# K projection of a DiT block: one more matmul ahead of two scale groups, and two K steps batch by batch

## The chip, the cores and the metric

The kernel runs on one core of a Trainium2 chip. The metric is device time in microseconds (us). "Span" is the time from the first to the last instruction in a profile; the timed figure is about 1.8 us longer (243.07 for a span of 241.26 in the profile of the kernel before).

## The reference, cut to what matters

```
B, N, D = 2, 256, 1152;  F = 4 * D                 # bf16
mod = (silu(c) @ w_mod).reshape(B, 6, 1, D)        # shift_a, scale_a, gate_a, shift_m, ...
h   = layernorm(x) * (1 + scale_a) + shift_a
qkv = (h @ wqkv)                                   # q, k, v;  2 heads of 576
...                                                # attention, wo, gate, second layernorm, MLP
```

Only the first microseconds matter here: `scale_a` is a small product of `silu(c)` with 1152 columns of `w_mod`, then the K projection needs `layernorm(x) * (1 + scale_a)`, transposed, as its moving operand. The shift is added later.

## The kernel before: the parts that the change touches

Tokens of both batches stand side by side: 512 columns, batch 0 in the first 256, batch 1 in the rest. The contraction of 1152 is cut into nine K steps of 128. Six PSUM accumulators `pk[0..5]` are filled step by step. The scale comes in groups of columns (0, 1, 2-3, 4-5, 6-7, 8), each from its own load.

```python
    for k0, k1 in SGROUPS:            # (0,2) (2,4) (4,6) (6,8) (8,9)
        nc.sync.dma_start(w_scale_a[...k0:k1...], ...)         # weights of the scale
        for a, z in [(0, 1), (1, 2)] if k0 == 0 else [(k0, k1)]:
            load_k(a, z, 0, KM1 * P)                           # weights of K, same rows
    load_k(0, KD, KM1 * P, D)
    # ... then w_shift_a, w_q, all on one queue
# [...]
    def scale_group(k0, k1, ...):     # 9 matmuls of 2 columns for each of the group's 128-column blocks
    def scale_add(pm, k0, k1, ...):   # VectorE: scale_a = pm + 1
    def both(pt, k):                  # scale the transposed block: batch 0 VectorE, batch 1 ScalarE
        for b, e in enumerate("da"):
            modulate(pt, 0, k, b, b * N, e)
    def k_step(k, c0=0, c1=T, m0=0, m1=KM1):
        for m in range(m0, m1):       # K step k, columns c0:c1, accumulators m0..m1-1
            nc.tensor.matmul(pk[m][:, c0:c1], w_k[:, k, m * P:(m + 1) * P], hT0[:, k, c0:c1], ...)
# [...]  K steps 0 to 2, scale groups 0 to 2-3
    for k in range(3, KD):
        split = 2 if k in (3, 5) else 0
        k_step(k, 0, T, 0, split)
        if k in (3, 5, 7):
            k1 = min(k + 3, KD)
            scale_add(scale_group(k + 1, k1), k + 1, k1)
        if k < KD - 1:
            both(transpose_x([k + 1], range(NT)), k + 1)
        k_step(k, 0, T, split)
# [...]  the last three column blocks of K, the shift, Q, attention, MLP
```

So the order on TensorE is: two matmuls of step 3, scale group 4-5, transposes of block 4, four matmuls of step 3, transposes of block 5, step 4, two matmuls of step 5, scale group 6-7, and so on.

## Time and profile before

| | |
|---|---|
| time, when the prediction was made | 242.99 us median of 3 (242.89 to 243.03) |
| span | 241.3 us |
| TensorE busy | 236.3 us, 98% |
| chain that ended last | 95% TensorE |

The page of the profile of before. The busy row of TensorE (PE), the clock in tenths over 40 slices, and the chain of waits that ended last:

```profile
span 241.3 us, 3993 instructions
...
PE 236.3 (98%) x1698; PEld 144.6 (60%) x1698; DVE 91.6 (38%) x194; ACT 60.1 (25%) x122; POOL 28.3 (12%) x47
...
PEclk9999999999999999999999999999999999999999
...
PE 95%; DMA 2%; DVE 1%; SPq 0%; issue 0%; DVEq 0%
```

A TensorE that is 98% busy is not necessarily without bubbles (short stretches in which the array has nothing to stream), because records of matmuls overlap: one of 512 columns is recorded as 379 ns long, but the next starts 216 ns later. What counts is the distance between starts. The timeline of TensorE in the kernel before (start in us, length in us, engine, line, what, how often) shows it. L250 are the scale groups, L267 transposes, L282 K steps:

```profile
9.30 0.60 PE L250 MATMUL pm<-sT,w_scale_a 128*128 128x2 bf16 x18
...
12.47 0.59 PE L250 MATMUL pt<-sT,w_scale_a 128*128 128x2 bf16 x18
...
15.44 0.59 PE L250 MATMUL pm<-sT,w_scale_a 128*128 128x2 bf16 x18
15.89 0.38 PE L267 MATMUL pt<-ident,xn 128*128 128x128 bf16 x4
16.11 1.03 PE L282 MATMUL pk<-big,w_k 128*128 128x512 bf16 x4
16.98 0.39 PE L267 MATMUL pt<-ident,xn 128*128 128x128 bf16 x4
17.25 1.89 PE L282 MATMUL pk<-big,w_k 128*128 128x512 bf16 x8
19.10 0.60 PE L250 MATMUL pm<-sT,w_scale_a 128*128 128x2 bf16 x18
19.56 0.38 PE L267 MATMUL pt<-ident,xn 128*128 128x128 bf16 x4
19.78 1.03 PE L282 MATMUL pk<-big,w_k 128*128 128x512 bf16 x4
20.64 0.39 PE L267 MATMUL pt<-ident,xn 128*128 128x128 bf16 x4
20.92 1.46 PE L282 MATMUL pk<-big,w_k 128*128 128x512 bf16 x6
22.21 0.37 PE L250 MATMUL pm<-sT,w_scale_a 128*128 128x2 bf16 x9
```

From 17.25 to 19.10 there are eight matmuls of 216 ns: 1.73 us of work in 1.85 us, so 0.12 us are lost ahead of group 6-7. Four transposes need 4 x 55 ns; from 16.98 to 17.25 and from 20.64 to 20.92 is 0.27 us, so 50 ns are lost ahead of K steps 4 and 6. What they wait for is told by the weight loads (PEld) of the same lines:

```profile
15.37 0.57 PEld L250 LDWEIGHTS <-w_scale_a 128*128 128x128 bf16 x18 [0.26 <-DMA w_scale_a<-in_w_mod_dram]
19.09 0.52 PEld L250 LDWEIGHTS <-w_scale_a 128*128 128x128 bf16 x18 [0.45 <-DMA w_scale_a<-in_w_mod_dram]
```

Both groups' weight loads wait for a transfer, but only the second wait costs the array anything: at 15.37 the matmul before it was still streaming.

The view of one load's line gives its issue and landing. For the load of group 6-7 in the kernel before:

```profile
L109 SPq DMA_DIRECT2D w_scale_a<-in_w_mod_dram x1: 469/469/469, 11.1 to 11.1; - x1
...
DMA to landing us min/median/max: 7.9/7.9/7.9
```

Issued at 11.1 us and landed 7.9 us later, at 19.05. (The trace has these in ns; 19.050.)

The waits at K steps 4 and 6 are for ScalarE, which scales batch 1 behind VectorE's batch 0:

```profile
16.34 0.35 DVE L273 TENSOR_SCALAR big<-pt,scale_a 128x256 bf16<-128x256 bf16 x1
```

```profile
16.72 0.47 ACT L274 ACTIVATE big<-pt,scale_a 128x256 bf16<-128x256 bf16 x1 [2.53 <-DVE big L273]
```

ScalarE starts 30 ns after VectorE ends, though it needs nothing that VectorE writes. Both read the same PSUM tile. The Trainium skill, "PSUM — Partial Sum Buffer", section "PSUM bank collisions raise a hardware error", says that no two engines may read one bank and quadrant at the same time and that schedulers put a dependency between them; the trace agrees here (16.69 to 16.72), and where the two batches lie in two tiles, at 13.30 and 13.36, the engines do overlap. Whether the wait is put in by tile or by bank, the trace doesn't tell.

### The profile page before, as it was taken

Reading aid. Unit: us, or ns where it says so; the run is one execution under the profiler, and the core shown is the slowest. Engines: PE = TensorE matmul, PEld = TensorE weight load, DVE = VectorE, ACT = ScalarE, POOL = GpSimd, SP = SyncE. Lnnn points to the kernel's source line nnn. Section 1 sums busy time; section 2 is a strip of 40 time slices with the busy share of each in tenths; the row PEclk is TensorE's granted clock in tenths of the full one; section 3 lists DMA queues with packets and bytes.
Section 4 is the critical chain, followed back from the end, with each engine's and each line's share of the span. In section 5 each row is a group of like instructions: output and inputs, shape, how many; then the busy total and the mean of one; then the engine's idle time right before and its main releaser. Section 6 shows DMA issues by size and latency. Waiting matters only on the chain.

```text
span 241.3 us, 3993 instructions
## 1 busy us (share of the span) xinstructions
PE 236.3 (98%) x1698; PEld 144.6 (60%) x1698; DVE 91.6 (38%) x194; ACT 60.1 (25%) x122; POOL 28.3 (12%) x47
## 2 busy tenths in 40 slices
PE   8899999999999999999999999999999999999994
PEld 5675444466667566888844444444666656666674
DVE  4842442319325678930002999950000000000001
ACT  6732322307215032770423333222000000000000
POOL 2300000001400324100000000001121111111111
PEclk9999999999999999999999999999999999999999
DMA  6999999998599994739999999999300000000000
GB/s 196 324 317 311 376 367 391 389 393 249 99 315 397 387 311 81 196 62 364 390 392 392 339 326 284 285 326 275 98 16 16 20 16 16 19 18 18 26 25 16
DMA packets 48925, 53.30 MB, mean 221 GB/s; under 512 B 9731, under 2 KB 36619, under 8 KB 48907
## 3 DMA queue, kind: packets, MB, share of 16 engines
q1 hardware_dynamic: 41312, 50.14, 62.6%
q10 hardware_dynamic: 7083, 1.72, 4.9%
q0 software_dynamic: 512, 1.19, 2.2%
q8 instruction: 13, 0.21, 0.4%
q14 instruction: 5, 0.04, 0.1%
HBM read 50.15 MB, written 1.19 MB: 213 GB/s over the span
## 4 chain that ended last, share of the span: by engine, by line
PE 95%; DMA 2%; DVE 1%; SPq 0%; issue 0%; DVEq 0%
PE pacc L806 29%; PE pacc L750 29%; PE pacc L697 7%; PE pacc L603 7%; PE pq L525 7%; PE pk L282 5%; PE pk L311 2%; DMA x_sb<-in_x_dram 2%; PE pa L644 2%; PE ps_s L560 2%; PE pn L420 2%; PE pt L267 1%; PE pm L250 1%; DVE stats L195 1%; PE pg L502 0%; SPq L88 0%
## 5 line engine op out<-in xcount | busy, mean ns | idle before, releaser
L750 PE MATMUL pacc<-hT,w_f 128*128 128x256 bf16 (+1 forms) x432 | 70.5, 326 | 0.0
L806 PE MATMUL pacc<-w_f,gT 128*128 128x384 bf16 (+2 forms) x468 | 70.5, 314 | 0.0
L806 PEld LDWEIGHTS <-gT 128*128 128x128 bf16 x468 | 44.4, 98 | 26.2
L750 PEld LDWEIGHTS <-w_f 128*128 128x128 bf16 x432 | 42.2, 98 | 27.6
L812 DVE TENSOR_TENSOR tmp<-pacc,gate 128x384 f32<-128x384 f32 (+2 forms) x13 | 6.9, 527 | 65.6 <-PE pacc L806 57.3
L782 ACT ACTIVATE gT<-pacc 128x512 bf16<-128x512 f32 x24 | 14.3, 597 | 32.7 <-PE pacc L750 32.7
L473 DVE SCALAR_TENSOR_TENSOR part<-w_gate_m,s,part 128x1152 f32<-128x1152 bf16 x16 | 21.4, 1414 | 0.0
L814 POOL TENSOR_TENSOR o_sb<-tmp,x 128x384 bf16<-128x384 f32 (+1 forms) x12 | 11.6, 971 | 53.9 <-DVE tmp L812 53.9
L697 PE MATMUL pacc<-w_o,big 128*128 128x384 bf16 x108 | 17.9, 326 | 0.0
L525 PE MATMUL pq<-hT,w_q 128*128 128x512 bf16 x81 | 17.8, 379 | 0.0
L603 PE MATMUL pacc<-w_v,hT 128*128 128x384 bf16 x108 | 17.7, 326 | 0.0
L603 PEld LDWEIGHTS <-hT 128*128 128x128 bf16 x108 | 10.5, 98 | 7.1 <-issue 0.3
L697 PEld LDWEIGHTS <-big 128*128 128x128 bf16 x108 | 10.4, 98 | 7.2 <-issue 0.4
L525 PEld LDWEIGHTS <-w_q 128*128 128x128 bf16 x81 | 7.9, 98 | 9.4
L282 PE MATMUL pk<-big,w_k 128*128 128x256 bf16 (+1 forms) x72 | 13.2, 325 | 0.0
L703 POOL TENSOR_TENSOR x<-tmp,x_sb 128x384 f32<-128x384 f32 x8 | 7.3, 911 | 26.3 <-DVE tmp L702 26.3
L471 DVE TENSOR_SCALAR part<-w_gate_m,s 128x1152 f32<-128x1152 bf16 x2 | 1.6, 818 | 22.2 <-DMA w_gate_m<-in_w_mod_dram 22.2
L495 POOL DMA_DIRECT2D gates_dram<-nat_v x2 | 1.1, 534 | 67.7 <-DVE nat_v L493 67.7
L282 PEld LDWEIGHTS <-w_k 128*128 128x128 bf16 x72 | 6.8, 97 | 3.5 <-issue 0.2
L771 ACT ACTIVATE gT<-pacc 128x512 bf16<-128x512 f32 x12 | 6.5, 597 | 9.1 <-PE pacc L750 9.1
L516 POOL DMA_DIRECT2D gates_dram<-nat x4 | 2.4, 596 | 49.8 <-DVE nat L513 48.4
L175 PE MATMUL pwarm<-zeros 128*128 128x256 f32 x18 | 6.7, 540 | 1.2 <-DVE eps_t L95 1.2
(106 smaller groups left out, 164.4 us busy)
## 6 DMA issues: line engine op xcount, KB each, us to landing
w_f<-in_w_fc_dram SPq DMA_DIRECT2D x12, 864.0 KB, 14.2
w_f<-in_w_fc_dram SPq DMA_DIRECT2D x3, 1728.0 KB, 10.1
w_f<-in_w_fc_dram SPq DMA_DIRECT2D x2, 2592.0 KB, 17.2
w_gate_a<-in_w_mod_dram SPq DMA_DIRECT2D x3, 864.0 KB, 14.4
w_v<-in_wqkv_dram SPq DMA_DIRECT2D x3, 864.0 KB, 15.4
w_o<-in_wo_dram SPq DMA_DIRECT2D x3, 864.0 KB, 14.7
w_shift_m<-in_w_mod_dram SPq DMA_DIRECT2D x3, 864.0 KB, 9.5
w_scale_m<-in_w_mod_dram SPq DMA_DIRECT2D x3, 864.0 KB, 15.8
```

The costliest lines, as they stand in the source:

```text
L175: nc.tensor.matmul(dst[:, 0:T // 2], zeros32[:, 0:P], zeros32, start=True, stop=True)
L282: nc.tensor.matmul(pk[m][:, c0:c1], w_k[:, k, m * P:(m + 1) * P], hT0[:, k, c0:c1], start=(k == 0 and c0 == 0), stop=(k == KD - 1), skip_g ...
L473: nc.vector.scalar_tensor_tensor(part[:, b, :], wg[:, k, :], s32[:, k, b:b + 1], part[:, b, :], op0=ALU.mult, op1=ALU.add,)
L525: nc.tensor.matmul(pq[m][:], w_q[:, k, m * P:(m + 1) * P], hT[:, k, :], start=(k == 0), stop=(k == KD - 1), skip_group_check=True,)
L603: nc.tensor.matmul(pacc[:], hT[:, k, t * P:(t + 1) * P], w_v[:, k, pnl * PW:(pnl + 1) * PW], start=(k == 0), stop=(k == KD - 1),)
L697: nc.tensor.matmul(pacc[:], aT[:, k, t * P:(t + 1) * P], w_o[:, k, c0:c1], start=(k == 0), stop=(k == KD - 1),)
L703: (nc.gpsimd if pool_add else nc.vector).tensor_tensor(x1[:, t, c0:c1], tmp[:], x_sb[:, t, c0:c1], op=ALU.add)
L750: nc.tensor.matmul(dst, w_f1[m // KD][:, k, ml * P:(ml + 1) * P], hT[:, k, c0:c1], start=start, stop=(k == KD - 1), **kw,)
L782: nc.scalar.activation(gT[:, m, :], pacc[:], ACT.Gelu_apprx_tanh)
L806: nc.tensor.matmul(pacc[:], gT[:, kk, t * P:(t + 1) * P], w_f2[j][:, r, c0 - n * PW:c0 - n * PW + cw], start=(kk == 0), stop=(kk == KF - 1),)
L812: nc.vector.tensor_tensor(tmp[:], pacc[:], gate_m[:, b, c0:c0 + cw], op=ALU.mult)
L814: (nc.vector if last else nc.gpsimd).tensor_tensor(o_sb[:], tmp[:], x1[:, t, c0:c0 + cw], op=ALU.add)
```

## The change

The intent: a third matmul of 216 ns goes ahead of groups 4-5 and 6-7, to cover the wait for their weights. That moves the scaling of the next block 216 ns closer to its use, so K steps 4 and 6 are cut in two: first all six accumulators for batch 0, which VectorE has ready early, then all six for batch 1.

```diff
     for k in range(3, KD):
-        split = 2 if k in (3, 5) else 0
+        split = 3 if k in (3, 5) else 0
         k_step(k, 0, T, 0, split)
         if k in (3, 5, 7):
             k1 = min(k + 3, KD)
             scale_add(scale_group(k + 1, k1), k + 1, k1)
         if k < KD - 1:
             both(transpose_x([k + 1], range(NT)), k + 1)
-        k_step(k, 0, T, split)
+        for c0, c1 in ((0, N), (N, T)) if k in (4, 6) else ((0, T),):
+            k_step(k, c0, c1, split)
```

## The prediction

> **What bounds the kernel now.** TensorE. The page gives PE 236.3 us busy of a 241.3 us span; the chain that ended last is 95% PE, 2% DMA, 1% DVE. The clock is full in all slices. Busy time hides bubbles, so I read starts of single matmuls in the timeline: a 512-column matmul starts 216 ns after its predecessor, a 256-column one 109-110 ns. This agrees with the Trainium skill, "TensorE: Matmul & The Clock Gate", section "Wait — 56ns, not 53.3ns?": columns / 2.4 GHz plus about 2.5 ns. Only three bubbles of K steps 3 to 8 can be won:
>
> - K step 4 starts at 17.25, 105 ns after the last transpose (55 ns is normal): its first matmul takes all 512 tokens and waits for ScalarE's scaling of batch 1, over at about 17.2. Loss about 50 ns.
> - Scale group 6-7 starts at 19.10, 341 ns after its predecessor (216 normal): its weights landed at 19.05. Loss 125 ns, and 10 ns in its first steps.
> - K step 6 starts at 20.92, as step 4: about 51 ns.
>
> Group 4-5 loses nothing: landed at 15.33, it started at 15.44, 216 ns after its predecessor; the 0.26 us idle shown there is of the weight load.
>
> **What the change does.**
> 1. One more 512-column matmul (216 ns) goes ahead of groups 4-5 and 6-7, one less follows. Work is moved, none added. Before 6-7 it covers the DMA wait: the group is then ready at about 19.16, behind the landing (19.05). Saves about 0.135 us. Before 4-5 there is nothing to cover.
> 2. Alone that would hurt K steps 4 and 6: scale add, VectorE scaling (0.35 us), then ScalarE scaling (0.47 us) come 216 ns later against TensorE, so batch 1 of step 4 is ready at about 17.45, against 17.20 for the array. Batch by batch, the first six matmuls need batch 0 alone (VectorE done at about 16.9) and run 0.66 us, when batch 1 has long been ready. Both 50 ns waits go.
> 3. The split makes twelve 256-column matmuls of six 512-column ones, twice: 6 x (2 x 109.2 - 215.8) = about 16 ns per step. The added weight loads of 98 ns hide behind 109 ns.
>
> Sum: -0.135 - 0.10 + 0.03 = about -0.2 us by scale group 8 (22.21 before, about 22.01 after).
>
> **Is it on the critical path?** Yes. Later loads land before they are needed: columns 6-8 of w_k at 24.57 (needed 25.03; slack 0.42 after the 43 ns from landing to load), first part of w_shift_a at 28.79 (needed 29.22; slack 0.39), w_q at 31.07 (needed 31.70). All exceed 0.2. From 30 us on TensorE has no wait over 0.1 us left, so the tail moves earlier whole. The loads before 30 us don't depend on TensorE.
>
> **Predicted: 242.80 us**, 8 in 10 within 242.60 to 243.05. Faster by over 2%: 0.5%; within 2%: 99%; slower: 0.5%.
>
> **Signs.** Right: scale group 6-7 begins 216 ns after its predecessor, without a wait for DMA; K steps 4 and 6 begin about 55 ns after the last transpose; PE has 1710 matmuls; span about 241.1. Wrong: a wait at batch 1, weight loads that show (over 110 ns per 256-column matmul), or a new DMA wait at w_k or w_shift_a.
>
> **What would make it wrong:** transfers landing 0.2 us later, which gives the gain back at 25 or 29 us; noise between runs (0.14 us) as large as the gain.

## The result

| | before | after |
|---|---|---|
| median (range), 6 executions each | 243.01 us (242.89 to 243.35) | 243.21 us (242.83 to 243.31) |
| span of the profile | 241.3 us | 241.4 us |

The ratio of after to before is 1.0003, with a 95% interval of 0.999 to 1.0016: the same. The predicted 242.80 us, and its range up to 243.05, were missed.

The page of after:

```profile
span 241.4 us, 4017 instructions
...
PE 235.6 (98%) x1710; PEld 145.3 (60%) x1710; DVE 91.5 (38%) x194; ACT 60.2 (25%) x122; POOL 28.3 (12%) x47
...
PE 95%; DMA 3%; SPq 1%; DVE 0%; issue 0%; DVEq 0%
```

TensorE has twelve more matmuls and 0.7 us less of recorded busy time, and yet the span is 0.1 us longer. The timeline of TensorE in after, for the same stretch and the start of the kernel:

```profile
9.58 0.60 PE L250 MATMUL pm<-sT,w_scale_a 128*128 128x2 bf16 x18 [0.27 <-DMA w_scale_a<-in_w_mod_dram]
...
12.83 0.59 PE L250 MATMUL pt<-sT,w_scale_a 128*128 128x2 bf16 x18
...
16.02 0.59 PE L250 MATMUL pm<-sT,w_scale_a 128*128 128x2 bf16 x18
16.47 0.38 PE L267 MATMUL pt<-ident,xn 128*128 128x128 bf16 x4
16.69 0.81 PE L282 MATMUL pk<-big,w_k 128*128 128x512 bf16 x3
17.34 0.39 PE L267 MATMUL pt<-ident,xn 128*128 128x128 bf16 x4
17.56 2.12 PE L282 MATMUL pk<-big,w_k 128*128 128x256 bf16 x15
19.52 0.59 PE L250 MATMUL pm<-sT,w_scale_a 128*128 128x2 bf16 x18
19.97 0.38 PE L267 MATMUL pt<-ident,xn 128*128 128x128 bf16 x4
20.19 0.81 PE L282 MATMUL pk<-big,w_k 128*128 128x512 bf16 x3
20.84 0.39 PE L267 MATMUL pt<-ident,xn 128*128 128x128 bf16 x4
21.06 1.47 PE L282 MATMUL pk<-big,w_k 128*128 128x256 bf16 x12
```

All three bubbles are gone. From 17.34 to 17.56 and from 20.84 to 21.06 is 0.22 us: four transposes and no wait. From 17.56 to 19.52 are twelve matmuls of 109 ns and three of 216 ns, 1.96 us of work in 1.96 us. The first matmul of scale group 8 started at 22.37, 22.21 in before. Everything else in this stretch starts later than in before, because the stretch itself began later: scale group 2-3 stands at 12.83, not 12.47. The weight loads of groups 4-5 and 6-7 in after wait for nothing:

```profile
15.80 0.72 PEld L250 LDWEIGHTS <-w_scale_a 128*128 128x128 bf16 x18
19.30 0.71 PEld L250 LDWEIGHTS <-w_scale_a 128*128 128x128 bf16 x18
```

The view of the load of group 6-7 in after:

```profile
L109 SPq DMA_DIRECT2D w_scale_a<-in_w_mod_dram x1: 470/470/470, 11.5 to 11.5; - x1
...
DMA to landing us min/median/max: 7.2/7.2/7.2
```

It was issued 0.37 us later than in before and landed 0.31 us earlier, at 18.74. So even without the change, group 6-7 would not have waited in this execution.

That suggests cutting each execution into three parts:

- **head**: from the start of the span to the first matmul of scale group 2-3. The two programs are the same up to here.
- **stage**: from there to the first matmul of scale group 8. The whole change lies here.
- **tail**: the rest.

| in ns, from the traces | head | stage | tail | span |
|---|---|---|---|---|
| before | 12469 | 9741 | 219054 | 241264 |
| after | 12830 | 9543 | 219054 | 241427 |

The tail is the same to the nanosecond. The stage is 198 ns shorter; the prediction had said 0.2 us. The head, which the change doesn't touch, is 361 ns longer. Of this, 274 ns are there already at scale group 0, which waited for its weights in after (the bracket at 9.58 above) and started at 9.30 in before: they landed at 9.15 in before and at 9.53 in after. The rest comes ahead of two transposes that wait for the normalised tile of x whose load landed last (7.21 in before, 7.57 in after).

### The profile page after: what moved, and what is told of

It reads as the page before. It is cut to its first block, busy times and chain, and to the rows that moved or that the text cites. A ratio compares the mean times of both kernels' runs of the same rounds, so it can differ in the third digit from the quotient of the medians.

```text
span 241.4 us, 4017 instructions
## 1 busy us (share of the span) xinstructions
PE 235.6 (98%) x1710; PEld 145.3 (60%) x1710; DVE 91.5 (38%) x194; ACT 60.2 (25%) x122; POOL 28.3 (12%) x47
## 4 chain that ended last, share of the span: by engine, by line
PE 95%; DMA 3%; SPq 1%; DVE 0%; issue 0%; DVEq 0%
PE pacc L807 29%; PE pacc L751 29%; PE pacc L698 7%; PE pacc L604 7%; PE pq L526 7%; PE pk L282 5%; DMA w_scale_a<-in_w_mod_dram 3%; PE pk L311 2%; PE pa L645 2%; PE ps_s L561 2%; PE pn L421 2%; PE pt L267 1%; PE pm L250 1%; SPq L88 1%; PE pg L503 0%; PE pt L250 0%
## 5 line engine op out<-in xcount | busy, mean ns | idle before, releaser
L282 PEld LDWEIGHTS <-w_k 128*128 128x128 bf16 x84 | 7.9, 98 | 2.5 <-issue 0.2
L703 DVE TENSOR_TENSOR tmp<-pacc,gate 128x384 f32<-128x384 f32 x12 | 6.6, 549 | 3.1 <-PE pacc L698 3.1
```

The costliest lines, as they stand in the source:

```text
L703: nc.vector.tensor_tensor(tmp[:], pacc[:], gate_a[:, b, c0:c1], op=ALU.mult)
```

## The experiments

Theory **chance**: the stage gains as predicted and the tail passes it on; head and landings differ from one execution to the next, whatever the kernel. Rival **layout**: the changed program itself makes the first transfers late, each time. Rival **no saving**: something behind the stage takes the gain back. Sixteen runs were made, in five calls; the kernels of one call ran on the same chip and share their runs of before. The five calls ran on five chips (numbers 10, 15, 8, 9 and 4 on record), so a difference between profiles of two calls can also be one between chips.

All profiles, in ns. "Gap" is the time from the landing of the weights of group 4-5 to that of group 6-7:

| run | head | stage | tail | gap | median us (executions timed) |
|---|---|---|---|---|---|
| before | 12469 | 9741 | 219054 | 3723 | 243.01 (6) |
| after | 12830 | 9543 | 219054 | 3038 | 243.21 (6) |
| e1 after again | 12474 | 9542 | 219047 | 3055 | 243.22 (6) |
| e2 before, copy | 12647 | 9831 | 219050 | 3880 | 243.16 (6) |
| e3 move only | 12365 | 10545 | 219047 | 4634 | 243.52 (6) |
| e4 batches only | 12819 | 9544 | 219065 | 3022 | 243.23 (6) |
| e5 before, group 6-7 without its wait | 12797 | 9609 | 219127 | 4343 | 243.31 (1) |
| e6 after, group 6-7 without its wait | 14851 | 9542 | 219062 | 3087 | 245.23 (1) |
| e7 after, one more early load | 12653 | 10430 | 219488 | 4477 | 244.34 (1) |
| e8 before, fewer warming matmuls | 12550 | 9606 | 219064 | 2985 | 242.99 (1) |
| e9 after, third | 12441 | 9719 | 219058 | 4188 | 243.08 (5) |
| e10 after, four ahead of 6-7 | 13001 | 9831 | 219059 | 4277 | 243.35 (5) |
| e11 the same, fewer warming matmuls | 12701 | 9544 | 219061 | 3043 | 243.04 (6) |
| e12 before, fewer warming matmuls | 12537 | 9607 | 219309 | 3058 | 243.07 (6) |
| e13 after, fewer warming matmuls | 12534 | 9543 | 219053 | 3080 | 242.91 (5) |
| e14 after, fourth | 12774 | 9686 | 219054 | 3868 | 243.40 (6) |
| e15, e16 as e13 | 12543, 12540 | 9541, 9545 | 219050, 219060 | 3097, 3086 | 242.95, 243.53 (6 each) |

### e1 and e2: both kernels again, unaltered

No edit.

> The changed kernel once more, unaltered. I cut an execution in three: head (span start to the first matmul of scale group 2-3; 12.47 us in the profile of before, 12.83 in that of after), stage (from there to the first matmul of scale group 8; 9.74 before, 9.54 after) and tail (219.05 in both, to the nanosecond). Theory 'chance' (the late head of after is scatter of the first transfers, that has nothing to do with the change): stage again about 9.54, tail 219.05, head anywhere from 12.3 to 12.9; over the five rounds the kernel is 0.07 to 0.2 us faster than before, ratio 0.9992 to 0.9997. Rival 'layout' (the longer program shifts the first transfers in every execution): head again about 12.8 and the time at or over that of before, ratio 1.000 to 1.001. Rival 'no saving' (something behind the stage takes it back): tail over 219.05.

> The kernel before, unaltered, against itself: what scatter alone does. Both theories: ratio 1.0000 within 0.0005. Stage about 9.74 where the head is about 12.4; where the head is late (12.8) the wait for the weights of scale group 6-7 shrinks, so that the stage is then 9.61 to 9.74. Tail 219.05. 'Chance' expects single times from 242.8 to 243.4 here too, with late ones among them; 'layout' expects nearly all within 242.85 to 243.1.

Measured: e1 has a head of 12.474 us, a stage of 9.542 and a tail of 219.047; e2 a head of 12.647, a stage of 9.831, a tail of 219.050. The ratios are 0.9994 (0.9977 to 1.0011) for e1 and 0.9993 (0.9977 to 1.001) for e2, a kernel against itself. Single times of the kernel before went from 242.83 to 243.91.

"Layout" is refuted as a delay in every execution: the same changed program has now a head as early as that of before, 12.474 against 12.469. "No saving" is refuted for the profiles: the tail did not grow. This pair is also the comparison that the result should have been, two profiles with the same head. The timeline of e1:

```profile
core 0 of [0], span 241.1 us
...
12.47 0.59 PE L250 MATMUL pt<-sT,w_scale_a 128*128 128x2 bf16 x18
...
22.02 0.37 PE L250 MATMUL pm<-sT,w_scale_a 128*128 128x2 bf16 x9
```

Before had 12.47 and 22.21, and a span of 241.3 us. By the traces 241.063 against 241.264 us: 0.201 us shorter, as predicted. But e2 also shows that the stage of before is not a constant: 9.83 instead of 9.74 us, and not 9.61 to 9.74 as I had expected, for its weights of group 6-7 landed at 19.32.

### e3 and e4: each half of the change alone

```diff
# e3, from the kernel before
-        split = 2 if k in (3, 5) else 0
+        split = 3 if k in (3, 5) else 0
# e4, from the kernel before
-        k_step(k, 0, T, split)
+        for c0, c1 in ((0, N), (N, T)) if k in (4, 6) else ((0, T),):
+            k_step(k, c0, c1, split)
```

> Only the first half of the change: three matmuls ahead of scale groups 4-5 and 6-7, K steps 4 and 6 whole. By the arithmetic of the traces K step 4 starts when ScalarE has scaled batch 1 (0.25 us behind the last transpose, not 0.05), K step 6 the same; the wait for the weights of group 6-7 (0.125) goes. Stage about 9.74 + 0.28 = 10.0 us, tail 219.05, so 0.2 to 0.3 us slower than before at an equal head: ratio 1.0008 to 1.0014. If the move were harmless by itself the stage would be 9.6.

> Only the second half: K steps 4 and 6 batch by batch, two matmuls ahead of the groups. The waits of 50 ns at K steps 4 and 6 go, 16 ns each are paid for the split, and the wait for the weights of group 6-7 stays and grows by what step 4 won. Stage about 9.71, tail 219.05: 0.03 us faster than before at an equal head, ratio 0.9998 within the scatter. If the batches alone carried the gain the stage would be 9.55.

The timeline of e3:

```profile
16.87 0.39 PE L267 MATMUL pt<-ident,xn 128*128 128x128 bf16 x4
17.36 2.10 PE L282 MATMUL pk<-big,w_k 128*128 128x512 bf16 x9
19.80 0.60 PE L250 MATMUL pm<-sT,w_scale_a 128*128 128x2 bf16 x18 [0.33 <-DMA w_scale_a<-in_w_mod_dram]
...
21.13 0.39 PE L267 MATMUL pt<-ident,xn 128*128 128x128 bf16 x4
21.62 1.46 PE L282 MATMUL pk<-big,w_k 128*128 128x512 bf16 x6
```

From 16.87 to 17.36 is 0.49 us where four transposes take 0.22: the wait for batch 1 is 0.27 us, as expected (0.25), and the same again at 21.13 to 21.62. The move alone is harmful, and the batches exist to pay for it. But the stage is 10.545 us, not 10.0: the weights of group 6-7 landed at 19.75, so the group waited for them although a third matmul stood ahead of it. In e4 the opposite happened: they landed at 18.74, nothing waited, and the stage was 9.544 us where I had expected 9.71. By the ratios (1.0009 and 0.9998, intervals of 0.0017 each way) neither differs from before.

The misses of e2, e3 and e4 have one cause, the landing of group 6-7. A small model, fitted after these runs to the two kernels, holds it. In before, group 6-7 starts at the later of (landing + 47 ns) and (head + 6503 ns), and group 8 starts 3113 ns after that. In after, it is head + 6688 ns, then 2855 ns. This gives 9.832 for e2 (measured 9.831) and 9.543 for e1 and after (9.542, 9.543). By the model the change is worth 73 ns when the landing is early, and up to 258 ns when it is late. The 0.2 us that I had predicted is its worth at one landing, that of the profile I read.

### e5 and e6: group 6-7 without its wait, wrong results on purpose

```diff
+    def src(j):
+        return j - 2 if j in (6, 7) else j
-    pm[:, j - k0, :], w_scale_a[:, k, j * P:(j + 1) * P], sT[:, k, 0:B],
+    pm[:, j - k0, :], w_scale_a[:, k, src(j) * P:(src(j) + 1) * P], sT[:, k, 0:B],
```

Group 6-7 reads the columns of group 4-5, which have landed. The outputs are wrong (relative error 0.055), as intended.

> Wrong result on purpose: the kernel before, whose scale group 6-7 reads the weight columns of group 4-5, that have landed. So its wait for its own weights is gone, nothing else changes. By the model that the six profiles fit (group 6-7 starts at the later of landing + 0.047 us and head + 6.50 us; 3.113 us from there to the end of the stage), the stage is 9.616 us whatever the scatter of the landing, tail 219.05. If something else than that landing made the stage of before vary (9.74, 9.83, 10.5 with the move alone), it stays over 9.65.

> Wrong result on purpose: the changed kernel with the same edit. By the model (head + 6.688, then 2.855) the stage is 9.543 us: with the landing out of the way the change is worth 0.073 us, the two waits at K steps 4 and 6 less the price of the split, and the other 0.125 us of the predicted saving was that execution's landing.

Measured: stages of 9.609 and 9.542 us. In e5 the unused weights landed as late as 19.85 us, and the stage no longer felt it. So the landing is what makes the stage of before vary, shown by taking it away; the rest of the change, the two waits of 50 ns less the price of the split, is worth 0.067 us.

e6 had an accident that is instructive. Its second tile of x landed at 5.55 us (4.3 to 4.9 in the other profiles), TensorE was idle for 2.49 us, and after that its clock fell to half. The timeline of e6:

```profile
9.63 0.62 PE L270 MATMUL pt<-ident,xn 128*128 128x128 bf16 x8 [2.49 <-DVE xn L235]
```

and its windows of 1 us (busy time of PE, PEld, DVE, ACT, POOL, then the granted clock, DMA share, GB/s):

```profile
11.00:12.00 1.00, 1.00 (x9) 0.70 (x7) 0.79 (x5) 0.79 (x4) 0.00 (x0) 0.64 1.08 344
12.00:13.00 1.00, 1.00 (x7) 0.79 (x6) 0.36 (x2) 0.00 (x0) 0.00 (x0) 0.50 1.15 308
13.00:14.00 1.00, 1.00 (x7) 0.67 (x6) 0.82 (x3) 0.47 (x1) 0.00 (x0) 0.50 1.16 306
```

The head was 14.85 us, 2.4 us late. Stage and tail were as ever, 9.542 and 219.062, and the time was 245.23 us. A late head is passed on whole; nothing behind it makes it good. (This is one execution of one run, so it is used for that alone.)

### e7 and e8: two attempts to move the transfers on purpose

```diff
# e7, from after
+    extra = act.tile([P, D], BF16, name="extra")
+    nc.sync.dma_start(extra[:], x_v[:, 0, 0, :])     # ahead of the first weights of the scale
# e8, from before
-    zeros = const.tile([P, T], BF16, name="zeros")
+    zeros = const.tile([P, 2 * T], BF16, name="zeros")
-            nc.tensor.matmul(dst[:, 0:T // 2], zeros32[:, 0:P], zeros32, start=True, stop=True)
+            nc.tensor.matmul(dst[:, 0:T], zeros32[:, 0:P], zeros32, start=True, stop=True)
-    warm(2, pwarm)   # and warm(7, pwarm)
+    warm(1, pwarm)   # and warm(3, pwarm)
```

> The changed kernel with one more load of 288 KB (x, into a tile that nobody reads) ahead of the first weights of the scale: it makes the first weights land later on purpose, by about 0.9 us at the 300 GB/s of these first microseconds (landing 9.1 to 9.5 becomes about 10.2). If a late first landing is passed on whole, the head becomes 13.3 to 13.7 us, stage 9.54, tail 219.05, and the time 243.7 to 244.2. If it is made good later, the stage or the tail shrinks and the time stays under 243.4.

> The kernel before, with the idle matmuls that warm the clock half as many and twice as wide: 20 instructions of TensorE fewer ahead of everything. Theory 'fetch': the 16 KB instruction transfer at 16.5 to 17.1 us (1.2 us long on one DMA engine) falls among the last packets of the weights of group 6-7 and delays that engine's share; it comes after a fixed number of TensorE instructions, so with 20 fewer it starts near 18 us, behind those packets, and group 6-7 lands 3.0 us after group 4-5 (not 3.7 to 4.6), so the stage is 9.616. Rival 'memory' (the late landing of group 6-7 is slow memory, not the instruction transfer): the transfer moves, the landing gap stays 3.7 or more in this two-matmul, unsplit kernel, stage 9.74 or more.

e7 failed in its aim: the first weights landed at 9.52 us, within the scatter of the others (8.81 to 9.69 over all profiles), and the head was 12.653. Its time of 244.34 came from elsewhere, a gap of 4.48 us ahead of group 6-7 (stage 10.430; the model says 10.42) and 0.43 us more at the end of the kernel, behind the last matmul. It does show that the changed kernel too waits when that landing is late enough.

e8 came out with an early landing and a stage of 9.606, but not for the reason given: the instruction transfer did not move behind the packets, it started earlier, at 16.19 us. So this run doesn't decide between "fetch" and "memory".

### e9, e10, e11: once more, with a fourth matmul, and with fewer instructions

```diff
# e10, from after
-        split = 3 if k in (3, 5) else 0
+        split = {3: 3, 5: 4}.get(k, 0)
# e11: e10 with the edit of e8
```

> The changed kernel unaltered, a third time, for more executions and another landing. The model (group 6-7 starts at the later of landing + 0.047 us and head + 6.688 us, 2.855 us from there to the end of the stage) gives its stage to 0.02 us, tail 219.05. By it the kernel is 0.07 us (early landing) to 0.26 us (late landing) faster than before at equal head and landing, and that drowns in single times that scatter over 0.7 us and more: ratio 0.9985 to 1.0005, unclear or same.

> The changed kernel with a fourth matmul of K step 5 ahead of scale group 6-7 (two behind it). By the model group 6-7 starts at the later of landing + 0.047 us and head + 6.904 us, then 2.639 us: stage 9.543 as after when the landing is early, up to 0.216 us shorter than after when it is late. K step 6 must still begin 55 ns behind the last transpose, for VectorE has batch 0 ready about 0.03 us before. If a wait for VectorE opens there, the stage is over 9.56 with an early landing and the theory of the slack at K step 6 is off. Time: as after, or a little under it.

> The same with the idle warming matmuls half as many and twice as wide, as in the run that had an early landing. If the 16 KB instruction transfer starts less than 1.4 us or more than 2 us after group 4-5 lands, the landing of 6-7 follows 4-5 by 3.0 us, if it starts 1.4 to 1.7 us after, by 3.7 us or more: so it was in all ten profiles. Stage 9.54 with an early landing, tail 219.05; the time then depends on the head alone: 242.8 to 243.3. Ratio to before 0.998 to 1.000.

In e9 the unaltered changed kernel met a late landing. The weight load and the landing in e9:

```profile
19.29 0.52 PEld L250 LDWEIGHTS <-w_scale_a 128*128 128x128 bf16 x18 [0.49 <-DMA w_scale_a<-in_w_mod_dram]
```

```profile
L109 SPq DMA_DIRECT2D w_scale_a<-in_w_mod_dram x1: 468/468/468, 10.9 to 10.9; - x1
...
DMA to landing us min/median/max: 8.3/8.3/8.3
```

The wait that the change was to remove was there again, and the stage was 9.719 us (the model says 9.71). e10 had an even later landing, 7.14 us after the head; its stage of 9.831 fits its model (9.82), where the model of after gives 10.04 for the same landing. So a fourth matmul is worth 0.21 us with a late landing and nothing with an early one (e11: 9.544). Ratios: 1.0000, 1.0005 and 1.0002, all the same as before.

### e12 to e16: does the timing of the instruction transfer decide, and does the gain reach the total?

e12 is e8 timed; e13, e15 and e16 are after with the edit of e8; e14 is after, a fourth time.

> The kernel before with half as many, twice as wide warming matmuls, now timed. In the two profiles with that edit the 16 KB instruction transfer started 0.8 and 1.1 us after the weights of group 4-5 landed, outside the 1.4 to 1.7 us that went with a late landing of 6-7 in seven of seven profiles. 'Fetch': again under 1.4 us, landing of 6-7 3.0 us behind 4-5, stage 9.61; and the times lose their late-landing part, so the median is 0.05 to 0.2 us under that of before. If the landing is late with the transfer outside 1.4 to 1.7 us, the theory falls.

> The changed kernel with the same edit. 'Fetch': transfer outside 1.4 to 1.7 us, landing early, stage 9.54, tail 219.05. Against the kernel before with the same edit it is then 0.07 us faster at an equal head, which the scatter of the head (12.4 to 13.0 us) hides: medians within 0.2 us of each other.

> The changed kernel unaltered, for more executions. Model: 0.07 us (early landing) to 0.26 us (late) faster than before in the mean of many executions. With this the changed kernel has about 22 executions and before about 45 with a scatter of 0.28 us each, so the difference of the means is known to 0.07 us: the model expects -0.07 to -0.2; a difference over +0.05 would say that the saving of the stage is lost somewhere that the profiles do not show.

> The changed kernel with half as many, twice as wide warming matmuls, once more, since its five executions (242.90 to 243.02 us, ratio 0.9986) were the only set that lay clear of before. If the edit really takes the late landings away, the median is again 242.9 to 243.0 and no more than one of six executions is over 243.3; stage 9.54, tail 219.05. If that set was luck, the times scatter as those of all other kernels (242.8 to 243.9, a third over 243.3) and the ratio is 0.999 to 1.001.

> The same file as the run before it, for six more executions: as there. Over both, if the edit works: median under 243.05 and at most two of twelve over 243.3; if luck, about four of twelve over 243.3.

The landing. In the packet records of the trace, a 16 KB transfer of the instruction queue starts at about 16.2 to 18.7 us and is recorded as one packet of 1.1 to 1.3 us. The Trainium skill, "Advanced Engine Details and Errata", section "ISA Cache", has cache lines of 16 KB for 256 instructions, which fits: later ones follow every 182 to 307 matmuls and weight loads of TensorE, 246 in the mean, in the four profiles that were counted. The skill's "DMA: Bandwidth & Descriptors", section "Why a DMA increments its semaphore by 16 and not by 1", says that a transfer has landed only when each of the up to 16 engines has finished its part. In e3, 97% of the packets of group 6-7 were in by 17.43 us and the last only at 19.15; in e11, with an early landing, by 17.74 and 18.03. In all eighteen profiles the landing came 0.5 to 0.9 us after the last packet, and the last 3% of the packets took 0.3 to 0.8 us where the landing was early and 0.8 to 1.7 us where it was late. So stragglers make the landing late. Through thirteen profiles the landing was late (a gap of 3.7 us or more) just when that transfer started 1.41 to 1.71 us after the landing of group 4-5. But in e14 it started 1.27 us after and the gap was 3.87, while in e1 it started 1.27 us after too and the gap was 3.06. By the test that I had set myself, the theory "fetch" falls as a rule. What makes the stragglers stays open.

The record shows one regularity more: all six profiles with the fewer, wider warming matmuls (e8, e11, e12, e13, e15, e16) had an early landing, a gap of 2.99 to 3.10 us, and only four of the twelve without them (after, e1, e4, e6). Chance alone would do that about once in 90 times, but this was noticed afterwards, and the times don't follow clearly: 29 timed executions with that edit have a mean of 243.18 us, 33 of before 243.26, a difference of -0.08 with a standard error of 0.08.

The total. e13 alone beat before clearly: ratio 0.9986 (0.9974 to 0.9997). Repeated, it didn't: e15 0.9988 (0.9972 to 1.0003), e16 1.0005 (0.9988 to 1.0023), with five of their twelve executions over 243.3 us, as "luck" had said. e12 and e14 had 0.9997 and 1.0008, the same as before. No version here beats both kernels.

e12 shows one more place where an execution can lose what it won. Its stage was early, 9.607, but the load of the shift weights landed at 29.37. The weight load of that line (L420) in e12:

```profile
29.41 0.60 PEld L420 LDWEIGHTS <-sT 128*32 128x32 bf16 x36 [0.68 <-DMA w_shift_a<-in_w_mod_dram]
```

and in the kernel before:

```profile
29.23 0.60 PEld L420 LDWEIGHTS <-sT 128*32 128x32 bf16 x36 [0.42 <-DMA w_shift_a<-in_w_mod_dram]
```

The 0.42 is there without any wait of the array (the same pattern at 37.2, where the weights had long landed, costs the same 309 ns between starts). The other 0.25 us is a true wait, and is the 0.25 us by which the tail of e12 is longer.

Over all rounds, the kernel before ran 56 times: mean 243.24 us, standard deviation 0.30, from 242.83 to 243.91. The changed kernel ran 23 times: mean 243.24, standard deviation 0.36, from 242.82 to 244.27. The difference of the means is 0.00 us with a standard error of 0.08. That is neither the -0.07 to -0.2 that I had expected in e14 nor the +0.05 that would have spoken for a loss. It is compatible with 0.07 us and speaks against 0.2 us in the mean. And of the two kernels no execution over 243.30 us has a trace, while 19 of the 56 and 7 of the 23 took longer than that: whether head, stage or tail makes these, no run here shows.

## Why the prediction was wrong, point by point

- **TensorE bounds the stage; three bubbles; their sizes.** Right. 50, 125 and 50 ns in the profile of before, all gone in after.
- **The move alone hurts, the batches pay for it.** Right, shown by e3: 0.27 us of wait at K steps 4 and 6 each. **The split costs about 16 ns per step and its weight loads stay hidden.** Right: 109 to 110 ns per matmul.
- **Sum of -0.2 us by scale group 8.** Right for the execution it was read from: 198 ns between the two profiles, 201 ns in the spans of before and e1, which have the same head. The model that carries it (landing, head) fits the other profiles of the two kernels to 0.02 us, and it forecast e5 and e6, where the wait was taken away, to 0.01 us.
- **It is on the critical path, the tail moves earlier whole.** Right in the profiles: the tails of before and the four profiles of after are 219.047 to 219.058.
- **"Predicted: 242.80 us", that is 242.99 - 0.2.** Here it failed. The step that failed is the one from 0.2 us in the stage to 0.2 us in the total: it took all that lies ahead of the change as fixed but for a "noise between runs (0.14 us)", and "Saves about 0.135 us" as a constant. In the profile of after the stage was 198 ns shorter, but the head was 361 ns longer, so that the span grew by 163 ns. Beside the result, before had 243.01 us in six executions (three of them those that I had predicted from), while four of the six executions of after took 243.20 to 243.31 and two 242.83 and 242.91; that after came out behind, and not ahead, is chance as far as the runs show. I took the range of three executions for the scatter of the kernel. It is 1.1 us wide in 56 executions, with a median of 243.22, so the base was 0.2 us too low for these; only 19 of the 56 executions of the unchanged kernel lie within the range of 242.60 to 243.05 that I gave to the changed one. And I took the landing of one profile (group 6-7 at 19.05) for a constant. It comes 3.0 to 4.6 us after that of group 4-5, and the 0.135 us term is nothing in an execution with an early landing and up to 0.185 us (6688 - 6503 ns, by the model) in one with a late one. In the very profile of after it landed at 18.74, and the term was zero there: the stage was shorter than that of the first profile, but before would have been shorter too.
- **"The loads before 30 us don't depend on TensorE."** True as far as the runs show, but it hid the point: they don't depend on TensorE and they don't repeat either. The head of after was 0.36 us longer because the first weights and a tile of x landed later, and the changed kernel had an early head again in e1.
- **New waits at w_k or w_shift_a.** None appeared in the four profiles of after. One of 0.25 us at w_shift_a appeared in e12, and a short one of 0.04 us in e5, so the slack of 0.39 us that I had counted on isn't safe either.

What stays open: what makes the last packets of a load late in some executions, what the executions over 243.30 us lose, and whether the saving of the stage lowers the mean time at all. The difference of the means is zero within 0.08 us; to see 0.07 us safely would need several times the executions.

## What to carry to other kernels

Before predicting a gain of 0.1% from one profile, ask which of its times would repeat: the ends of matmuls do, to a few ns, but the landings of the first loads here moved by 0.6 us (first weights) and 1.3 us (group 6-7) between four executions of the same program. Cut the span at points that the change does not touch, compare head, stage and tail apart, and compare profiles with the same head; a gain in the stage can be exact there and still be invisible in the total. And a wait for a transfer is worth covering only by what it costs over many executions, not in the one that was looked at.

## What the Trainium skill lacked or had wrong

- "TensorE: Matmul & The Clock Gate", section "What's actually happening": the clock is said to fall after at least one idle window of about 3.4 us. In e6, the only one of the sixteen profiles with a record of the clock in which it fell before the last matmul, the longest idle time was 2.49 us: the matmuls ran at half speed for 3.41 us, from 11.28 to 14.69 us, beginning 1.6 us after they had resumed at 9.63. Idle times up to 1.7 us at the same place in the other profiles didn't lower it. An estimate from these traces, with windows of 3.41 us counted from the first record of full clock: the window that ended at the fall was idle for 1.77 us, and no other from there to the last matmul, in any of these profiles, for more than 1.16 us. So a window that is idle in part was enough, in one execution; where the limit lies is not shown.
- The same page, section "Wait — 56ns, not 53.3ns?": agrees, 215 to 216 ns at 512 columns and 109 to 110 ns at 256.
- "DMA: Bandwidth & Descriptors" doesn't say how far the landing of one and the same load scatters from execution to execution. Here the 576 KB load of group 6-7 landed 3.0 to 4.6 us after that of group 4-5 in eighteen profiles of nearly the same program, and 3.0 to 4.2 us in four of exactly the same.
- "Advanced Engine Details and Errata", section "ISA Cache", has the 16 KB cache line, and neither it nor another page says how long the transfer of one takes: in these traces it is recorded as a packet of 0.9 to 1.5 us (2.5 us once), amid the kernel's own loads. Whether it delays them stayed open.
